# 1/den of each head spread over its 32 feature partitions by a DMA from a DRAM table, in place of selector matmuls

## The chip, the cores and the metric

The kernel runs on one core of one Trainium2 chip. The metric is the device time of one execution in microseconds (us). The core has five engines that run their own instruction streams: PE (TensorE, matmuls), DVE (VectorE), ACT (ScalarE), POOL (GpSimd) and SP (SyncE, which here only issues DMAs). PEld is PE's weight load, which overlaps the matmuls. SPq is the stream of DMA issues of SP.

## What is computed

One transformer block on x of 2048 tokens by 1024 features, with a modulation from a conditioning vector: a linear-attention half and a gated FFN half, each behind a layer norm.

```python
q, k, v = split(h @ wqkv)                    # 32 heads of 32 features
phi = lambda t: where(t > 0, t + 1, exp(t)) + 1e-06
kv  = einsum('bhsd,bhse->bhde', phi(k), v)
z   = einsum('bhsd->bhd', phi(k))
num = einsum('bhqd,bhde->bhqe', phi(q), kv)
den = einsum('bhqd,bhd->bhq', phi(q), z)[..., None] + 1e-06
x   = x + ga * ((num / den) @ wo)
h   = layernorm(x) * (1 + cb) + sb
x   = x + gb * ((gelu(h @ w_gate) * (h @ w_up)) @ w_down)
```

The change is about the division by `den`: one number for each of 32 heads and 2048 tokens.

## The kernel before

The tokens are cut into 16 chunks of 128 and into 4 supergroups (sg) of 512. phi(q) lies transposed in `PQ[sg]`: partitions are features, 128 at a time, so that one of the 8 groups g holds 4 heads of 32 features each, and the free axis is 512 tokens. The output projection reads `PQ`, 128 features by 128 tokens, against `W2`, which is kv times wo. So 1/den must multiply `PQ` before `wo_chunk` (L934) reads it, and 1/den of a head has to stand on all its 32 feature partitions.

Every engine runs a list of instructions in the order in which the program text adds them; a small scheduler (`Sched`, L145) adds the waits from byte ranges that are read and written, in SBUF and in PSUM. SP's DMAs take 8 lanes in turn: a DMA waits for the one issued 8 before it on SP to have landed (`Sched.dma`, L184). An instruction that waits holds everything behind it on its engine.

The stretch that the change touches lies between the last k/v chunk and the FFN:

1. `den(0, 3)` (L858): 32 small matmuls give den of supergroups 0 and 1, for 32 heads by 256 tokens on 32 partitions, four times (i = 0 to 3 is the 256-token half). DVE adds 1e-6 (L868) and takes the reciprocal (L869) into `RDC` [128, 256] f32. POOL splits it into a bf16 high part and a bf16 rest, `RDHL` (L870, L871).
2. Eight rounds u: `q_next` is a q block of 8 matmuls (L654) of supergroup 3, evacuated by ACT's exp (L602) and two DVE instructions (L603, L605), out of two PSUM banks in turn; `w2_pair(u)` is two matmuls (L851) and a copy by ACT (L853). After rounds 0, 2, 4 and 5 comes `bcast(0, r)` (L874): 16 matmuls (L879) of a 0/1 selector `SEL` with `RDHL` that write 1/den on 128 partitions of PSUM banks 4 to 7, and four DVE multiplications `pq_scale` (L888, L892) of `PQ` by PSUM.
3. Twelve output chunks `wo_chunk(0)` to `wo_chunk(11)`, 16 matmuls each (L939), into banks 0/1 or 2/3 in turn (chunk 0: 6/7), each evacuated by one DVE addition into x (L946, here "x1"). A chunk's matmuls wait for the x1 of the chunk two before it. After chunk 0 comes `den(1, 4)` for supergroups 2 and 3, after chunks 2, 3, 5 and 6 `bcast(1, r)`. `ln2_a` (L963) normalises chunks 0 to 3 on ACT with small POOL instructions, and transposes each into `H2[0]` by a DMA from SP (L529, "T2"). After chunk 9, `mod2` (L554) modulates `H2[0]` on DVE in 16 instructions (L539).
4. The FFN of supergroup 0 starts: 28 feature chunks of 16 matmuls (L1005, L1008) in 14 pairs fp, the last four output chunks being put after pairs 1 to 4 by `hooks`. The weights come by `stream_pair` (L928: `WG`, `WU`, 512 KB each, three slots), issued two pairs ahead.

SP's list in this stretch: wg and wu of pairs 0 and 1 (slots which held `WO`, so each waits for some `w2_pair`), `wd_dma` 4, 5 and 6 (L924, 1 MB each, down-projection weights), T2 of chunks 0 to 3, wg and wu of pair 2, and so on. `wd_dma` 0 to 3 follow in the FFN, after pairs 5 to 8.

`SEL` is built once at the start of the program by `sel_build` (L693): 32 matmuls and one ACT copy, amid `warm` matmuls (L667) on zeros, while the first inputs are still on their way.

Of the kernel before, what the change touches and what calls it, by code (L numbers as in the profile page):

```python
# [10 lines left out]
P = 128  # L11
# [39 lines left out]
OFF_VS = OFF_PK + 5 * 2048  # L51
OFF_MS3 = OFF_VS + 3 * NG * KV_SLOT * 2
OFF_XH2 = OFF_MS3 + 8192
OFF_RDHL = OFF_WS + 16384
assert OFF_XH2 + 2048 <= OFF_WS
OFF_GAB = OFF_CONST
OFF_GBB = OFF_CONST + 4096
# [157 lines left out]
def bass_adaLN_cond__linear_attn_block__geglu_ffn__prompt_kernel(  # L215
# [11 lines left out]
):  # L227
    bf16, f32, i32 = dt.bfloat16, dt.float32, dt.int32
    scr_row = nc.dram_tensor("scr_row", [2, 4, 512], f32).ap()
    with ExitStack() as es:  # L230
        es.enter_context(nc.allow_non_contiguous_dma(reason="1024 modulation values, laid out by partition"))
        arena = es.enter_context(nc.sbuf_tensor("arena", [P, ARENA_BYTES], dt.uint8, align_bytes=64))
# [4 lines left out]
        def at(name, shape, dty, off):  # L237
            return nc.alloc_sbuf_tensor_at(name, shape, dty, offset=ABASE + off, align_bytes=4)
# [20 lines left out]
        WMQ = [at(f"wmq{i}", [P, NDC, 2, 256], bf16, MSO[i]) for i in range(4)]  # L259
        WARM = at("warm", [P, 512], bf16, OFF_GUH)  # L260
        WO = at("wo", [P, NDC, D], bf16, OFF_WS)
        RDHL = at("rdhl", [P, 2, 2, SGW // 2], bf16, OFF_RDHL)
        YT = at("yT", [P, NFC, SGW], bf16, OFF_YT)
        WG = [at(f"wg{i}", [P, NDC, 256], bf16, OFF_WS + i * 8192) for i in range(3)]
        WU = [at(f"wu{i}", [P, NDC, 256], bf16, OFF_WS + i * 8192 + 4096) for i in range(3)]
# [18 lines left out]
        _o = OFF_SMALL  # L284
        _small = {}
        for name, shape, dty, sz in [
            ("ident", [P, P], bf16, 256), ("bmask", [P, P], bf16, 256), ("bm32", [P, NG, NH], bf16, 512), ("sel", [P, NG, P], bf16, 2048),
            ("z32", [P, NG, NH], bf16, 512), ("rdc", [P, SGW // 2], f32, 1024),
            ("silr", [P, NDC, 32], bf16, 512),
            ("c8", [NDC, P], bf16, 256), ("cT", [P, NDC], f32, 64), ("chalf", [P, NDC], f32, 64),  # L290
            ("thc", [P, NDC], f32, 64), ("siluT", [P, NDC], bf16, 64), ("modt", [P, 16], f32, 64), ("add4", [P, 4], f32, 64),
            ("sbT", [P, NDC], f32, 64), ("cb1T", [P, NDC], f32, 64),
            ("cbT", [P, NDC], f32, 64), ("zcols", [P, NG], f32, 64), ("neghalf", [P, 1], f32, 64),
            ("st", [P, NCH, 12], f32, NCH * 48), ("mv", [P, NCH, 2], f32, NCH * 8),
            ("rs", [P, NCH], f32, 64), ("nm", [P, NCH], f32, 64), ("ve", [P, NCH], f32, 64),
        ]:
            SMO[name] = _o
            SMSZ[name] = sz
            _small[name] = at(name, shape, dty, _o)
            _o += sz  # L300
        assert _o <= OFF_CONST + SZ_CONST, (_o, OFF_CONST + SZ_CONST)
        IDENT, BMASK, BM32, Z32, SEL = (_small[k] for k in ("ident", "bmask", "bm32", "z32", "sel"))
        RDC = _small["rdc"]
        SILR, C8, CT, CHALF, THC, SILUT = (_small[k] for k in ("silr", "c8", "cT", "chalf", "thc", "siluT"))
        SBT, CB1T, CBT, ZCOLS = (_small[k] for k in ("sbT", "cb1T", "cbT", "zcols"))
# [4 lines left out]
        def r_sm(name):  # L310
            return [(SMO[name], SMO[name] + SMSZ[name], name)]
# [43 lines left out]
        def r_wm(i):  # L355
            return [(MSO[i], MSO[i] + 8192, f"wmst{i}")]

        def r_rdhl(sg, k):
            return [(OFF_RDHL + (sg * 2 + k) * 512, OFF_RDHL + (sg * 2 + k + 1) * 512, "rdhl")]

        R_SEL = r_sm("sel")

        def r_yt(fc, s0=0, s1=SGW):
            return [(OFF_YT + (fc * SGW + s0) * 2, OFF_YT + (fc * SGW + s1) * 2, "yT")]
# [18 lines left out]
        def pr(b):  # L383
            return [(b * 2048, (b + 1) * 2048)]
# [20 lines left out]
        def pset_writer(b, o):  # L405
            for t_ in pr(b):
                sch.ps.set_writer(t_[0], t_[1], o)
# [4 lines left out]
        def gop(fn, **kw):  # L412
            d_ = [last_g[0]] if last_g[0] is not None else []
            last_g[0] = sch.op(G, fn, deps=d_, **kw)
# [9 lines left out]
        bm32f = BM32.ap().rearrange("p a b -> p (a b)")  # L424
        for k in range(HPG):
            gop(lambda e, k=k: e.memset(BMASK[32 * k:32 * (k + 1), 32 * k:32 * (k + 1)], 1.0), wr=r_sm("bmask"))
            gop(lambda e, k=k: e.memset(bm32f[32 * k:32 * (k + 1), k:k + 36 * 7 + 1:36], 1.0), wr=r_sm("bm32"))


        sch.dma(Q, lambda e: e.dma_start(C8[:], c_v), wr=r_sm("c8"), note="c8")  # L430
# [236 lines left out]
        def warm(n, bank=None):  # L667
            for _ in range(n):
                sch.op(T, lambda e: e.matmul(PS(0 if bank is None else bank), WARM[:, 0:P], WARM[:, :], start=bank is not None,
                                             stop=bank is not None, skip_group_check=True),  # L670
                       rd=R_WARM, pwr=pr(bank) if bank is not None else (), note="warm")
# [18 lines left out]
                        kv_mm(c_, "k", jg, b, [dc])  # L690


        def sel_build():  # L693
            o = None
            for g in range(NG):
                b, c0 = 2 + g // 4, (g % 4) * P
                for j in range(4):
                    o = sch.op(T, lambda e, g=g, b=b, c0=c0, j=j: e.matmul(
                        ps_all[32 * j:32 * (j + 1), b * 512 + c0:b * 512 + c0 + P], BM32[:, g, :], IDENT[:, :], start=True, stop=True),
                        rd=r_sm("bm32") + r_sm("ident"), pwr=pr(b) if g % 4 == 0 and j == 0 else (), note=f"sel{g}.{j}")  # L700
                pset_writer(b, o)
            sch.op(A, lambda e: e.activation(SEL[:].rearrange("p a b -> p (a b)"), ps_all[:, 1024:2048], ACTF.Copy),
                   prd=pr(2) + pr(3), wr=R_SEL, note="sel")

        warm(9, 7)
        sel_build()
        ln1_bn(0, 0)
        ln1_bn(0, 1)
        ln1_fin(0)
# [148 lines left out]
        def den(pr_, b):  # L858
            o = None
            for g in range(NG):  # L860
                for i in range(4):
                    sg, t0 = 2 * pr_ + i // 2, (i % 2) * HW
                    o = sch.op(T, lambda e, g=g, i=i, sg=sg, t0=t0: e.matmul(  # L863
                        ps_all[32 * i:32 * (i + 1), b * 512:b * 512 + HW], Z32[:, g, :], PQ[sg][:, g, t0:t0 + HW],
                        start=(g == 0), stop=(g == NG - 1)),
                        rd=r_sm("z32") + r_pq(sg, g, g + 1, t0, t0 + HW), pwr=(pr(b) if g == 0 else ()), note=f"den{pr_} {g}.{i}")
            pset_writer(b, o)
            sch.op(V, lambda e: e.tensor_scalar(RDC[:, :], PS(b, 0, HW), 1e-6, None, op0=ALU.add), prd=pr(b), wr=r_sm("rdc"), note=f"dene{pr_}")  # L868
            sch.op(V, lambda e: e.reciprocal(RDC[:, :], RDC[:, :]), rd=r_sm("rdc"), wr=r_sm("rdc"), note=f"rden{pr_}")  # L869
            o = sch.op(G, lambda e: e.tensor_copy(RDHL[:, pr_, 0, :], RDC[:, :]), rd=r_sm("rdc"), wr=r_rdhl(pr_, 0), deps=[last_g[0]], note=f"rdhi{pr_}")  # L870
            last_g[0] = sch.op(G, lambda e: e.tensor_tensor(RDHL[:, pr_, 1, :], RDC[:, :], RDHL[:, pr_, 0, :], ALU.subtract),  # L871
                   rd=r_sm("rdc") + r_rdhl(pr_, 0), deps=[o], wr=r_rdhl(pr_, 1), note=f"rdlo{pr_}")

        def bcast(pr_, r):  # L874
            o = [None] * 4
            for gi in range(2):
                for k in range(2):
                    for i in range(4):
                        o[i] = sch.op(T, lambda e, gi=gi, k=k, i=i: e.matmul(  # L879
                            PS(4 + i, gi * HW, (gi + 1) * HW), SEL[32 * i:32 * (i + 1), 2 * r + gi, :], RDHL[32 * i:32 * (i + 1), pr_, k, :],  # L880
                            start=(k == 0), stop=(k == 1)),
                            rd=R_SEL + r_rdhl(pr_, k), pwr=(pr(4 + i) if gi == 0 and k == 0 else ()), note=f"bc{pr_} {r}.{gi}.{k}.{i}")
            for i in range(4):
                pset_writer(4 + i, o[i])
            for i in range(4):
                pq_scale(pr_, r, i)

        def pq_scale(pr_, r, i):  # L888
            sg, t0 = 2 * pr_ + i // 2, (i % 2) * HW
            ap = PQ[sg][:, 2 * r:2 * r + 2, t0:t0 + HW]  # L890
            rng = r_pq(sg, 2 * r, 2 * r + 2, t0, t0 + HW)
            sch.op(V, lambda e: e.tensor_tensor(ap, ap, PS(4 + i).rearrange("p (a b) -> p a b", a=2), ALU.mult),  # L892
                   prd=pr(4 + i), rd=rng, wr=rng, note=f"pqs{pr_}.{r}.{i}")

        q_todo += [(NSG - 1, qc) for qc in range(NG)]
        qn = [0]
# [11 lines left out]
        q_evac(*first_q)  # L908
        q_next()
        den(0, 3)  # L910
        kvbd()
        q_next()
        q_next()
        kvt()
        for u in range(NG):
            q_next()
            w2_pair(u)
            if u in (0, 2, 4, 5):
                bcast(0, (0, 2, 4, 5).index(u))
        assert not q_todo  # L920

        wd_q = [0]
# [53 lines left out]

        stream_pair(0, 0)
        stream_pair(0, 1)
        for q in (4, 5, 6):
            wd_dma(q)  # L980
        for c_ in range(12):
            wo_chunk(c_, 6 if c_ == 0 else 2 * (c_ % 2))
            if c_ == 0:
                den(1, 4)
            if c_ in (2, 3, 5, 6):
                bcast(1, (2, 3, 5, 6).index(c_))
            if c_ < 4:
                ln2_a(c_, False)
            if c_ == 9:
                mod2(0, 2)  # L990
                mod2(2, 2)
# [57 lines left out]

        for ci in range(CPG):  # L1050
            hook(0, 1 + ci, lambda ci=ci: wo_chunk(12 + ci, 6))
        for q in range(4):
            hook(0, 5 + q, lambda q=q: wd_dma(q))
        for sg in range(NSG):
# [94 lines left out]
```

## Time and profile before

| what | value |
|---|---|
| median of 8 runs | 849.27 us (849.08 to 849.71) |
| the profiled execution's own time | 849.27 us |
| its span, first to last instruction | 847.5 us |
| granted TensorE clock | 1.00 of full speed |
| DVE busy | 492.1 us (58%) |
| ACT busy | 295.8 us (35%) |
| POOL busy | 25.4 us (3%) |
| DMA, mean over the span | 123 GB/s, 104.06 MB |
| selector matmuls, 128 | 5.5 us busy, 270 ns each |
| `pq_scale`, 32 | 19.8 us busy, 680 ns each |
| reciprocal, 2 | 3.5 us busy, 1753 ns each |
| first `den` matmul, first `wo_chunk` matmul, first FFN matmul | 178.7, 205.2 and 250.3 us from the span's start |

Times of the profile are from the start of the span. In a line of the timeline the columns are start, duration of the whole group, engine, line, operation, names, shape and count, and in brackets how long the engine had been idle and what ended that. Matmuls are pipelined: the mean of one (379 ns for 512 columns) is longer than the step from one start to the next (0.216 us), so costs on PE are taken from starts. In a line by windows, "DMA share" is the mean busy share of the 16 DMA engines (it can pass 1 in a short window) and the last column is GB/s.

### The profile page before, as it was taken

The page shows a single profiled execution, that of the slowest core. Times are in us where ns is not written, and L with a number is a line of the kernel's source. Part 1 is how long each engine was busy: PE and PEld are TensorE (multiplying, and loading weights), DVE is VectorE, ACT ScalarE, POOL GpSimd, SP SyncE. Part 2 cuts the span into 40 slices and gives each one's busy share as a digit, 9 for nine tenths or more (in the row PEclk, how much of TensorE's full clock was granted, in tenths as well). Part 3 has the DMA queues.
Part 4 walks back from the last instruction along what each step waited for, and adds up shares of the span by engine and source line. Part 5 has one row for each costly group of instructions (what it writes and reads, how often), then busy time and mean ns, then how long its engine had stood idle before and what let it go on. Part 6 is the DMA issues. An engine that isn't in the chain of part 4 may idle for free.

```text
span 847.5 us, 11598 instructions
## 1 busy us (share of the span) xinstructions
PE 840.8 (99%) x4386; PEld 390.2 (46%) x4386; DVE 492.1 (58%) x883; ACT 295.8 (35%) x484; POOL 25.4 (3%) x68
## 2 busy tenths in 40 slices
PE   8999999999999999999999999999999999999998
PEld 4454444444444444444444444444444444444445
DVE  5676767778665555563456555445666535556512
ACT  3343333344504345430254452035444204544300
POOL 2000000000200000010000001000000000000000
PEclk9999999999999999999999999999999999999999
DMA  9991823004423388341455534055553305555000
GB/s 276 358 285 26 261 56 95 13 2 152 135 63 100 101 253 242 100 100 37 112 150 151 154 108 104 21 147 156 154 150 100 75 19 155 150 151 148 6 19 26
DMA packets 179927, 104.06 MB, mean 123 GB/s; under 512 B 32536, under 2 KB 171928, under 8 KB 179872
## 3 DMA queue, kind: packets, MB, share of 16 engines
q1 hardware_dynamic: 179872, 103.33, 43.8%
q8 instruction: 35, 0.57, 0.3%
q14 instruction: 20, 0.16, 0.1%
HBM read 92.28 MB, written 4.21 MB: 114 GB/s over the span
## 4 chain that ended last, share of the span: by engine, by line
PE 97%; DMA 1%; SPq 1%; DVE 1%; issue 0%; ACT 0%; ACTq 0%
PE ps_all L1033 23%; PE ps_all L1008 23%; PE ps_all L1005 23%; PE ps_all L613 13%; PE ps_all L939 7%; PE ps_all L654 6%; DMA wk<-in_A_wqkv_dram 1%; PE ps_all L635 1%; PE ps_all L879 0%; SPq L444 0%; PE ps_all L585 0%; SPq L433 0%; PE ps_all L851 0%; DVE pq L892 0%; PE ps_all L863 0%; PE ps_all L566 0%
## 5 line engine op out<-in xcount | busy, mean ns | idle before, releaser
L1005 PE MATMUL ps_all<-h2T,wg 128*128 128x512 bf16 x896 | 339.6, 379 | 0.0
L1008 PE MATMUL ps_all<-h2T,wu 128*128 128x512 bf16 x896 | 339.6, 379 | 0.0
L1033 PE MATMUL ps_all<-wd,yT 128*128 128x512 bf16 (+1 forms) x924 | 194.1, 373 | 0.0
L1016 ACT ACTIVATE q<-ps_all 128x512 f32<-128x512 f32 x112 | 66.9, 597 | 235.3 <-PE ps_all L1005 234.0
L1033 PEld LDWEIGHTS ps_all<-wd,yT 128*128 128x128 bf16 x924 | 90.4, 98 | 103.3
L1005 PEld LDWEIGHTS ps_all<-h2T,wg 128*128 128x128 bf16 x896 | 87.7, 98 | 105.8 <-issue 0.2
L1008 PEld LDWEIGHTS ps_all<-h2T,wu 128*128 128x128 bf16 x896 | 87.7, 98 | 105.6
L1018 DVE SCALAR_TENSOR_TENSOR ww<-q,ps_all 128x512 f32<-128x512 f32 x112 | 77.0, 688 | 92.5 <-ACT guh L1017 92.5
L1021 DVE SCALAR_TENSOR_TENSOR ww<-th,guh 128x512 f32<-128x512 f32 x112 | 77.5, 692 | 77.9 <-ACT th L1020 77.9
L1020 ACT ACTIVATE th<-ww 128x512 f32<-128x512 f32 x112 | 70.5, 629 | 84.4 <-DVE ww L1018 84.4
L1023 DVE TENSOR_TENSOR yT<-ww,ps_all 128x512 bf16<-128x512 f32 x112 | 76.9, 686 | 3.8
L1038 DVE TENSOR_TENSOR ps_all<-ps_all,gbb 128x512 f32<-128x512 f32 (+1 forms) x33 | 22.5, 682 | 94.8 <-PE ps_all L1033 94.8
L1017 ACT ACTIVATE guh<-ps_all 128x512 f32<-128x512 f32 x112 | 66.3, 592 | 0.0
L602 ACT ACTIVATE eb<-ps_all 128x512 f32<-128x512 f32 x64 | 37.5, 601 | 81.0 <-PE ps_all L613 38.5
L613 PE MATMUL ps_all<-wk,h1T 128*128 128x512 bf16 x256 | 58.2, 379 | 0.9 <-DMA wk<-in_A_wqkv_dram 0.9
L654 PE MATMUL ps_all<-h1T,wq 128*128 128x512 bf16 x256 | 58.9, 379 | 0.0
L613 PE MATMUL ps_all<-wv,h1T 128*128 128x512 bf16 x256 | 57.7, 379 | 0.0
L939 PE MATMUL ps_all<-w,pq 128*128 128x512 bf16 x256 | 56.9, 379 | 0.0
L603 DVE TENSOR_SCALAR eb<-eb 128x512 f32<-128x512 f32 x64 | 27.1, 424 | 32.9 <-ACT eb L602 32.4
L613 PEld LDWEIGHTS ps_all<-wk,h1T 128*128 128x128 bf16 x256 | 24.7, 98 | 30.4 <-DVE h1T L539 2.1
L613 PEld LDWEIGHTS ps_all<-wv,h1T 128*128 128x128 bf16 x256 | 25.0, 98 | 29.7 <-DVE eb L603 0.2
L939 PEld LDWEIGHTS ps_all<-w,pq 128*128 128x128 bf16 x256 | 24.6, 98 | 30.1 <-issue 1.1
(88 smaller groups left out, 409.4 us busy)
## 6 DMA issues: line engine op xcount, KB each, us to landing
wg<-in_B_w_gate_dram SPq DMA_DIRECT2D x56, 512.0 KB, 4.0
wu<-in_B_w_up_dram SPq DMA_DIRECT2D x56, 512.0 KB, 5.2
wmst<-in_w_mod_dram SPq DMA_DIRECT2D x8, 1024.0 KB, 11.9
wd<-in_B_w_down_dram SPq DMA_DIRECT2D x7, 1024.0 KB, 7.6
wmq<-in_w_mod_dram SPq DMA_DIRECT2D x8, 512.0 KB, 6.9
out_dram<-xall SPq DMA_DIRECT2D x31, 128.0 KB, 1.7
xall<-in_A_x_dram SPq DMA_DIRECT2D x3, 1024.0 KB, 11.6
wk<-in_A_wqkv_dram SPq DMA_DIRECT2D x4, 512.0 KB, 7.7
```

What stands on the lines that cost most here:

```text
L613: o = sch.op(T, lambda e, dc=dc: e.matmul(PS(bank), H1[sg][:, dc, ci * P:(ci + 1) * P], W_[:, dc, jg * 512:(jg + 1) * 512], start=(dc == 0 ...
L654: o = sch.op(T, lambda e, dc=dc: e.matmul(PS(b), WQ[:, dc, qc * P:(qc + 1) * P], H1[sg][:, dc, :], start=(dc == 0), stop=(dc == NDC - 1)), ...
L939: last[half] = sch.op(T, lambda e, g=g, half=half: e.matmul(PS(b0 + half), PQ[sg][:, g, ci * P:(ci + 1) * P], W2[:, g, half * 512:(half + ...
L1005: og = sch.op(T, lambda e, dc=dc: e.matmul(PS(bg), WG[slot][:, dc, e_ * P:(e_ + 1) * P], H2[sg][:, dc, :], start=(dc == 0), stop=(dc == ND ...
L1008: ou = sch.op(T, lambda e, dc=dc: e.matmul(PS(bu), WU[slot][:, dc, e_ * P:(e_ + 1) * P], H2[sg][:, dc, :], start=(dc == 0), stop=(dc == ND ...
L1016: sch.op(A, lambda e: e.activation(Q1[j][:, :], PS(bg), ACTF.Square, scale=math.sqrt(GELU_A)), prd=pr(bg), wr=rq, note=f"q1 {fc}")
L1017: ogh = sch.op(A, lambda e: e.activation(GUH[j][:, :], PS(bg), ACTF.Copy, scale=0.5), prd=pr(bg), wr=rg, note=f"gh {fc}")
L1018: sch.op(V, lambda e: e.scalar_tensor_tensor(WW[j][:, :], Q1[j][:, :], 1.0, PS(bg), op0=ALU.add, op1=ALU.mult), rd=rq, prd=pr(bg), wr=rw, ...
L1020: sch.op(A, lambda e: e.activation(TH[j][:, :], WW[j][:, :], ACTF.Tanh, scale=GELU_C), rd=rw, wr=rt, note=f"th {fc}")
L1021: sch.op(V, lambda e: e.scalar_tensor_tensor(WW[j][:, :], TH[j][:, :], 1.0, GUH[j][:, :], op0=ALU.add, op1=ALU.mult), rd=rt + rg, wr=rw, n ...
L1023: sch.op(V, lambda e: e.tensor_tensor(YT[:, fc, :], WW[j][:, :], PS(bu), ALU.mult), rd=rw, prd=pr(bu), wr=r_yt(fc), note=f"yT {fc}")
L1033: o = sch.op(T, lambda e, b=b, fc=fc, c0=c0, c1=c1, n=n: e.matmul(PS(b, 0, n), YT[:, fc, ci * P:(ci + 1) * P], WDT[fc // 4][:, fc % 4, c0:c1],
```

## The change

- `SEL`, `sel_build`, `RDHL`, its two POOL instructions and `bcast` with its 128 selector matmuls go. Three more `warm` matmuls stand where `sel_build` was.
- After each reciprocal, SP stores `RDC` (128 KB, f32) to a DRAM table `scr_rd` (one such store for supergroups 0 and 1, one for 2 and 3). The heads' order within den's 32 partitions is changed (the memset of `BM32`) so that the 8 groups' values of one position k in the group lie in one row of 8 KB.
- `rb_load(sg)`: eight DMAs, for each 256-token half h and each k one that reads a row of 8 KB 32 times into 32 partitions of `RB[sg % 2]` (f32; 256 KB for each DMA, 2 MB for each supergroup). The two buffers lie where `WV` was, and where `PK` and `VS` were. Only the first DMA of a half carries the waits of the buffer; all eight wait for the store.
- `pq_scale(sg, h)`: four DVE multiplications of `PQ` (bf16) by `RB` (f32, in SBUF), of the same 512 elements for each partition as before, but ordered by half and supergroup: those of supergroup 0 after rounds 3 and 5, of 1 after chunks 0 and 1, of 2 after chunks 4 and 5, of 3 after chunks 6 and 7. They wait for all four DMAs of their half.
- On SP: store 0, `rb_load(0)`, `rb_load(1)`, then wg and wu of pairs 0 and 1, store 1, `rb_load(2)`, T2 of chunk 0, `rb_load(3)`, T2 of chunks 1 to 3, wg and wu of pair 2. `wd_dma` 4, 5 and 6 move into the FFN, after pairs 1, 2 and 3.

```diff
-        def sel_build():
...
-        warm(9, 7)
-        sel_build()
+        warm(12, 7)
...
-            o = sch.op(G, lambda e: e.tensor_copy(RDHL[:, pr_, 0, :], RDC[:, :]), rd=r_sm("rdc"), wr=r_rdhl(pr_, 0), deps=[last_g[0]], note=f"rdhi{pr_}")
-            last_g[0] = sch.op(G, lambda e: e.tensor_tensor(RDHL[:, pr_, 1, :], RDC[:, :], RDHL[:, pr_, 0, :], ALU.subtract),
-                   rd=r_sm("rdc") + r_rdhl(pr_, 0), deps=[o], wr=r_rdhl(pr_, 1), note=f"rdlo{pr_}")
-
-        def bcast(pr_, r):
...
+            o_s = sch.dma(Q, lambda e: e.dma_start(scr_rd[2 * pr_:2 * pr_ + 2].rearrange("s f k (g t) -> (s f k g) t", g=NG), RDC[:, :]),
+                          rd=r_sm("rdc"), note=f"rden{pr_}.st")
+            o_rd[pr_] = o_s
...
+        def rb_load(sg):
+            i = sg % 2
+            for h in range(2):
+                made = []
+                for k in range(HPG):
+                    made.append(sch.dma(Q, lambda e, h=h, k=k: e.dma_start(
+                        RB[i][32 * k:32 * (k + 1), h, :, :].rearrange("p a b -> p (a b)"),
+                        scr_rd[sg, h, k:k + 1, :].to_broadcast([32, NG * HW])),
+                        wr=r_rb(i, h) if k == 0 else (), deps=made[0].deps if k else [o_rd[sg // 2]], note=f"rb{sg}.{h}.{k}"))
+                rb_ops[sg, h] = made
+
+        def pq_scale(sg, h, gs=((0, 2), (2, 4), (4, 6), (6, 8))):
+            i, t0 = sg % 2, h * HW
+            for g0, g1 in gs:
+                ap = PQ[sg][:, g0:g1, t0:t0 + HW]
+                rng = r_pq(sg, g0, g1, t0, t0 + HW)
+                sch.op(V, lambda e, ap=ap, i=i, h=h, g0=g0, g1=g1: e.tensor_tensor(ap, ap, RB[i][:, h, g0:g1, :], ALU.mult),
+                       rd=rng + r_rb(i, h, g0, g1), wr=rng, deps=rb_ops[sg, h], note=f"pqs{sg}.{h}.{g0}")
...
         den(0, 3)
+        rb_load(0)
+        rb_load(1)
         kvbd()
...
-            if u in (0, 2, 4, 5):
-                bcast(0, (0, 2, 4, 5).index(u))
+            if u in (3, 5):
+                pq_scale(0, (u - 3) // 2)
...
         stream_pair(0, 1)
-        for q in (4, 5, 6):
-            wd_dma(q)
         for c_ in range(12):
             wo_chunk(c_, 6 if c_ == 0 else 2 * (c_ % 2))
             if c_ == 0:
                 den(1, 4)
-            if c_ in (2, 3, 5, 6):
-                bcast(1, (2, 3, 5, 6).index(c_))
+                rb_load(2)
+            if c_ in (0, 1):
+                pq_scale(1, c_)
+            if c_ == 1:
+                rb_load(3)
+            if c_ in (4, 5, 6, 7):
+                pq_scale(2 + (c_ - 4) // 2, c_ % 2)
             if c_ < 4:
                 ln2_a(c_, False)
...
+        for q in range(3):
+            hook(0, 1 + q, lambda q=q: wd_dma(4 + q))
```

More of the change, by code (lines that the diff above doesn't have):

```diff
@@ L53 @@
 OFF_XH2 = OFF_MS3 + 8192
-OFF_RDHL = OFF_WS + 16384
+OFF_RB = [OFF_WD + 16384, OFF_YT]
 assert OFF_XH2 + 2048 <= OFF_WS
@@ L229, in bass_adaLN_cond__linear_attn_block__geglu_ffn__prompt_kernel @@
     scr_row = nc.dram_tensor("scr_row", [2, 4, 512], f32).ap()
+    scr_rd = nc.dram_tensor("scr_rd", [NSG, 2, HPG, NG * (SGW // 2)], f32).ap()
     with ExitStack() as es:
@@ L261, in bass_adaLN_cond__linear_attn_block__geglu_ffn__prompt_kernel @@
         WO = at("wo", [P, NDC, D], bf16, OFF_WS)
-        RDHL = at("rdhl", [P, 2, 2, SGW // 2], bf16, OFF_RDHL)
+        RB = [at(f"rb{i}", [P, 2, NG, SGW // 2], f32, OFF_RB[i]) for i in range(2)]
         YT = at("yT", [P, NFC, SGW], bf16, OFF_YT)
@@ L286, in bass_adaLN_cond__linear_attn_block__geglu_ffn__prompt_kernel @@
         for name, shape, dty, sz in [
-            ("ident", [P, P], bf16, 256), ("bmask", [P, P], bf16, 256), ("bm32", [P, NG, NH], bf16, 512), ("sel", [P, NG, P], bf16, 2048),
+            ("ident", [P, P], bf16, 256), ("bmask", [P, P], bf16, 256), ("bm32", [P, NG, NH], bf16, 512),
             ("z32", [P, NG, NH], bf16, 512), ("rdc", [P, SGW // 2], f32, 1024),
@@ L301, in bass_adaLN_cond__linear_attn_block__geglu_ffn__prompt_kernel @@
         assert _o <= OFF_CONST + SZ_CONST, (_o, OFF_CONST + SZ_CONST)
-        IDENT, BMASK, BM32, Z32, SEL = (_small[k] for k in ("ident", "bmask", "bm32", "z32", "sel"))
+        IDENT, BMASK, BM32, Z32 = (_small[k] for k in ("ident", "bmask", "bm32", "z32"))
         RDC = _small["rdc"]
@@ L356, in r_wm, with r_rb @@
             return [(MSO[i], MSO[i] + 8192, f"wmst{i}")]
-        def r_rdhl(sg, k):
-            return [(OFF_RDHL + (sg * 2 + k) * 512, OFF_RDHL + (sg * 2 + k + 1) * 512, "rdhl")]
-        R_SEL = r_sm("sel")
+        def r_rb(i, h, g0=0, g1=NG):
+            return [(OFF_RB[i] + (h * NG + g0) * 1024, OFF_RB[i] + (h * NG + g1) * 1024, f"rb{i}")]
         def r_yt(fc, s0=0, s1=SGW):
@@ L426, in bass_adaLN_cond__linear_attn_block__geglu_ffn__prompt_kernel @@
             gop(lambda e, k=k: e.memset(BMASK[32 * k:32 * (k + 1), 32 * k:32 * (k + 1)], 1.0), wr=r_sm("bmask"))
-            gop(lambda e, k=k: e.memset(bm32f[32 * k:32 * (k + 1), k:k + 36 * 7 + 1:36], 1.0), wr=r_sm("bm32"))
+            gop(lambda e, k=k: e.memset(bm32f[32 * k:32 * (k + 1), 8 * k:8 * k + 33 * 7 + 1:33], 1.0), wr=r_sm("bm32"))
         sch.dma(Q, lambda e: e.dma_start(C8[:], c_v), wr=r_sm("c8"), note="c8")
@@ L690, in k_part @@
                         kv_mm(c_, "k", jg, b, [dc])
-        def sel_build():
[L694 to L703, printed above, removed]
-        warm(9, 7)
-        sel_build()
+        warm(12, 7)
         ln1_bn(0, 0)
@@ L874, in bcast @@
-        def bcast(pr_, r):
[L875 to L893, printed above, removed]
+            o_s = sch.dma(Q, lambda e: e.dma_start(scr_rd[2 * pr_:2 * pr_ + 2].rearrange("s f k (g t) -> (s f k g) t", g=NG), RDC[:, :]),
+                          rd=r_sm("rdc"), note=f"rden{pr_}.st")
@@ new lines, in den @@
+            o_rd[pr_] = o_s
+        o_rd = {}
+        rb_ops = {}
+        def rb_load(sg):
[8 more added lines that the diff above has]
+                rb_ops[sg, h] = made
```

## The prediction

> **What bounds the kernel now.** I read first the busy times, then the chain of waits, then PE's timeline over the stretch that the change touches.
>
> ```profile
> PE 840.8 (99%) x4386; PEld 390.2 (46%) x4386; DVE 492.1 (58%) x883; ACT 295.8 (35%) x484; POOL 25.4 (3%) x68
> PE 97%; DMA 1%; SPq 1%; DVE 1%; issue 0%; ACT 0%; ACTq 0%
> ```
>
> PE works 99% of the span, and 97% of the chain that ends last is PE. So what is taken from PE's list shortens the run one for one, until another engine or a transfer is late. Next, how PE's list passes one selector round among the q blocks, the one that waits, and one among the output chunks:
>
> ```profile
> 195.84 0.59 PE L851 MATMUL ps_all<-wo,kvt 128*128 128x512 bf16 x2
> 196.36 0.62 PE L879 MATMUL ps_all<-rdhl,sel 32*128 32x256 bf16 x16
> 196.91 1.90 PE L654 MATMUL ps_all<-h1T,wq 128*128 128x512 bf16 x8
> 198.65 0.59 PE L851 MATMUL ps_all<-wo,kvt 128*128 128x512 bf16 x2
> 199.17 0.28 PE L879 MATMUL ps_all<-rdhl,sel 32*128 32x256 bf16 x2
> 199.72 0.28 PE L879 MATMUL ps_all<-rdhl,sel 32*128 32x256 bf16 x1 [0.27 <-DVE pq L892]
> 200.32 0.61 PE L879 MATMUL ps_all<-rdhl,sel 32*128 32x256 bf16 x13 [0.32 <-DVE pq L892]
> 200.86 1.90 PE L654 MATMUL ps_all<-h1T,wq 128*128 128x512 bf16 x8
> 216.74 0.62 PE L879 MATMUL ps_all<-rdhl,sel 32*128 32x256 bf16 x16
> 217.28 3.63 PE L939 MATMUL ps_all<-w,pq 128*128 128x512 bf16 x16
> 233.06 17.44 PE L939 MATMUL ps_all<-w,pq 128*128 128x512 bf16 x80
> 250.33 0.38 PE L1005 MATMUL ps_all<-h2T,wg 128*128 128x512 bf16 x1
> ```
>
> Step by starts: a w2 pair with no round behind it takes 0.43 (the next q block starts 0.43 after it), with a round 1.07. An output chunk takes 3.45 (17.27 for five of them, 233.06 to 250.33). The fourth round also waits for PSUM that the multiplications of the round before still read.
>
> **What goes from PE.** Rounds after u = 0, 2 and 4: 0.64 each; after u = 5: 2.21 - 0.43 = 1.78; four among the chunks, 0.65 each by the starts (for instance 216.74 - 209.72 - 6.91 + 0.54). Together 1.92 + 1.78 + 2.62 = 6.3 us.
>
> **The start.** sel_build's 32 matmuls take 0.97 of PE (6.21 to 7.18); three warm ones take 0.65 (0.216 each, as after 8 us) to 1.28 (0.427 each, as before 6 us), so between -0.3 and +0.3. I take 0: PE waits at 18.33 for a transfer of wk anyway; uncovered it would be those 0.3. ACT's copy of 1.02 us goes, which had nothing late behind it.
>
> **Multiplications.** The nearest row with the same operands (bf16 by f32, both in SBUF) is the fold of wo, twice as long; half of 1218 is 609, and the present row is 680. I take 680 each, and 2.5 for four in a row as now (2.47). Count 32 stays; only the order changes.
>
> ```profile
> L821 DVE TENSOR_TENSOR wo<-wo,gab 128x1024 bf16<-128x1024 bf16 x8 | 9.4, 1218 | 0.0
> L892 DVE TENSOR_TENSOR pq<-pq,ps_all 128x512 bf16<-128x512 bf16 x32 | 19.8, 680 | 0.0
> L946 DVE TENSOR_TENSOR xall<-ps_all,xall 128x1024 bf16<-128x1024 f32 x16 | 19.6, 1222 | 14.4 <-PE ps_all L939 14.4
> ```
>
> After u = 3 the four lie on DVE from about 194.3 to 196.8; the q evacuation behind them frees its bank at 197.9, while PE wants it at 197.1 and goes on at 198.0: a new stall of 0.9. So if no transfer is late, chunk 0 starts at 205.19 - 3.70 + 0.9 = 202.4, and the FFN at 202.4 + 12 x 3.45 + 1.07 (den) = 244.9 in place of 250.33: **5.4 us less**, the most that there is.
>
> **The transfers.** Eight MB of broadcast are new on SP's queue. The nearest rows are the broadcasts of gab and gbb (DRAM rows read by 128 partitions):
>
> ```profile
> gab<-scr_row SPq DMA_DIRECT2D x1, 512.0 KB, 10.4
> gbb<-scr_row SPq DMA_DIRECT2D x1, 512.0 KB, 8.7
> 98.00:100.00 2.00, 2.00 (x11) 0.90 (x10) 1.39 (x3) 0.60 (x1) 0.00 (x0) 1.00 1.05 426
> ```
>
> Their landing times hold a queue of weights ahead of them; the rate when they flow is 426 GB/s. Each new transfer reaches a quarter of the partitions. If that costs nothing, the rate is 426; if rate goes with partitions reached, 426/4 = 107. No row has a large transfer to fewer than 128 partitions. I take the middle in ratio, **213 GB/s** (an estimate): 1 MB, a half of a supergroup, in 4.92 us.
>
> [...]
>
> Now the chain, at 213. The reciprocal ends at 181.03 + 1.75 = 182.78; store to the next DMA's issue 1.9 (for mrow and sbT: 119.36 to 121.29), so 184.8; first bytes 1.4 after an issue (wg: 189.39 to about 190.8), 186.2. The halves of supergroups 0 and 1 flow until 191.1, 196.0, 201.0 and 205.9, and land 0.6 later (as T2 did: flow to 220.4, landed 221.0). They are due at 194.3, 199.0, 209.7 and 213.4: in time, by 2.4 or more. Behind them on SP's queue wg and wu of pairs 0 and 1, 2 MB at 300 GB/s (1.03 MB in 3.4 us from 237), 7.0 us, to 212.9. Behind those store 1, issued at 209.7 already (chunk 0 ends 205.85, den 0.99, then x1, the addition and 1.75): landed at 213.9. Supergroup 2 flows from 215.4 to 225.2, its halves landing at 220.9 and 225.8, due 222.2 and 226. Then T2 of chunk 0, 1.4; supergroup 3 from 226.6 to 236.5, landing at **232.1 and 237.1**. Due are they at 229.7 and, after the shift, 235.8.
>
> So DVE waits twice, and behind it stand the x1 additions that free PSUM. The multiplications end at 234.6, x1 of chunk 7 at 235.8, chunk 9 starts at 236.0 (PE ready 234.55). The second set ends at 239.6, x1 of chunk 8 at 240.8, chunk 10 runs from 241.0, chunk 11 to 247.9, and the FFN starts at 248.0. T2 of chunks 1 to 3 queue behind: 240.7, landed 241.3; mod2 (4.2) is due at 242.0: hidden, by under 1 us. Two other waits of these DMAs do not bind: the buffers are free before the loads come (multiplications of supergroup 0 done at 201.5, load at 214.0; of 1 at 215.9, load behind T2), and a lane's DMA of eight before has landed while seven others, 8.6 us of flow, are still queued. Gain 250.33 - 248.0 = **2.3 us**.
>
> The 8 MB are paid in full along this chain, so the FFN starts at 248.0 + 39.4 x (213/rate - 1): break-even is 201 GB/s, the full 5.4 is had from 231 on.
>
> **At nothing.** wd 4 to 6 leave a queue that moved 402 GB/s from 212 to 216 and go behind pairs 1 to 3: the windows from 264 to 295 move some 100 GB/s, and pairs 6 and 7 carry the same 1 MB beside wg and wu in 7 us (306 GB/s, PE never idle). Were that cover gone, each would cost up to its 2.6 us at 402. POOL's split (1.07 twice) is off the path.
>
> **The sum.** The profiled execution took 849.27 (span 847.5 and 1.8 around it), which is also the median. 849.27 - 2.3 = **847.0**.
>
> **Rivals.**
> The first: transfers as fast as gab's, over 231 GB/s. For it: the sources repeat in both, and rows of 8 KB are longer than gab's 2 KB. Against: only 32 partitions. 849.27 - 5.4 = 843.9.
> The second, slower: under 201 GB/s the last half of supergroup 3 holds DVE at its multiplication, x1 of chunk 8 behind it and PE behind that, for longer than the selector rounds cost. For it: 32 short transfers instead of few long ones, and the queue never drains between 186 and 240. At 175: 256.6, so 849.27 + 6.2 = 855.5.
> The third: rate by partitions, 107. FFN at 287, 886. [...]
>
> **Chances.** Forecast (201 to 231 GB/s, 843.9 to 849.3) 0.43; as fast as gab 0.13; 150 to 201 (849.3 to 863) 0.36; below that 0.08. A measurement here tells 0.2%, 1.7 us, from no change: that is 210 GB/s upward and 193 downward. Of the forecast 0.29 lies above 210 and 0.14 within; of the slower rival 0.06 within. Faster 0.42, same 0.20, slower 0.38. The range runs from 843.7 to 858 (167 GB/s), leaving out the quarter rate and the low end of the second rival; the forecast's own is 843.9 to 849.3.
>
> **What would show it.** PE passes u = 5 with no wait and chunk 0 starts near 202.4; L879 is gone. In windows from 187 to 205 the DMA rate is near 213, with share near 1. Half 1 of supergroup 3 lands near 237; DVE waits for it; chunk 9 or 10 waits for x1; the FFN starts near 248. I am wrong if the rate is elsewhere, if the first halves are late among the q blocks, if T2 is late for mod2, or if the FFN's first pairs wait for weights.

## The result, and the profile after

| | before | after |
|---|---|---|
| median | 849.39 us (35 runs, 848.68 to 852.61) | 847.08 us (13 runs, 846.58 to 849.17) |
| profiled execution, own time and span | 849.27, 847.5 us | 848.07, 846.3 us |
| first `den` matmul | 178.72 us | 179.77 us |
| first FFN matmul | 250.33 us | 249.03 us |
| from the one to the other, "the stretch" | 71.61 us | 69.26 us |

The ratio is 0.9972, with a 95% interval of 0.9965 to 0.998: 2.3 us less, and 847.0 was forecast. The interval alone leaves 1.7 to 3.0 us, so that the two agree within 0.1 us is closer than the runs can tell.

The stretch is the better measure of what the change does. In the profiled execution of after, PE waited 1.03 us at 34.69 for a VectorE instruction, where before has no wait, and everything behind it lies some 1 us later. Such differences at the start come and go: among the eleven kernels from after to e10 (ten have after's start, e8 the old one) the first `den` matmul lies between 177.90 and 180.30 us. Below, 1.05 us (179.77 - 178.72) is taken off times of after where they are set against the forecast.

The page of after, busy times and chain of waits:

```profile
PE 835.6 (99%) x4229; PEld 387.3 (46%) x4229; DVE 492.0 (58%) x883; ACT 295.0 (35%) x483; POOL 24.5 (3%) x64
PE 93%; DMA 4%; DVE 2%; SPq 1%; issue 1%; ACT 0%; DVEq 0%; ACTq 0%
```

PE has 5.2 us less to do, and the span did not become shorter by as much. The chain tells why: DMA holds 4% of it where it held 1%, DVE 2% where it held 1%. The end is no longer set by PE alone. PE's timeline over the stretch (start, duration of the group, engine, line, operation, count, and in brackets the idle time before it and what ended it):

```profile
197.74 0.59 PE L837 MATMUL ps_all<-wo,kvt 128*128 128x512 bf16 x2
198.99 1.90 PE L653 MATMUL ps_all<-h1T,wq 128*128 128x512 bf16 x8 [0.66 <-DVE pq L604]
200.73 0.59 PE L837 MATMUL ps_all<-wo,kvt 128*128 128x512 bf16 x2
...
203.32 3.62 PE L928 MATMUL ps_all<-w,pq 128*128 128x512 bf16 x16
...
207.86 27.80 PE L928 MATMUL ps_all<-w,pq 128*128 128x512 bf16 x128
237.22 3.63 PE L928 MATMUL ps_all<-w,pq 128*128 128x512 bf16 x16 [1.56 <-DVE xall L935]
242.11 7.08 PE L928 MATMUL ps_all<-w,pq 128*128 128x512 bf16 x32 [1.27 <-DVE xall L935]
249.03 0.38 PE L997 MATMUL ps_all<-h2T,wg 128*128 128x512 bf16 x1
```

No selector matmul stands between a w2 pair and what follows. In their place are three waits: 0.66 among the q blocks, and 1.56 and 1.27 before chunks 9 and 10, where PE wants a PSUM bank that x1 (now L935) has not yet emptied. What x1 stands behind is seen on DVE, in the multiplications of supergroups 2 and 3:

```profile
223.02 2.49 DVE L879 TENSOR_TENSOR pq<-pq,rb 128x512 bf16<-128x512 bf16 x4
...
227.54 2.50 DVE L879 TENSOR_TENSOR pq<-pq,rb 128x512 bf16<-128x512 bf16 x4 [0.90 <-DMA rb<-scr_rd]
...
233.53 2.50 DVE L879 TENSOR_TENSOR pq<-pq,rb 128x512 bf16<-128x512 bf16 x4 [2.35 <-DMA rb<-scr_rd]
...
238.42 2.50 DVE L879 TENSOR_TENSOR pq<-pq,rb 128x512 bf16<-128x512 bf16 x4 [1.26 <-DMA rb<-scr_rd]
```

DVE waits 4.5 us in all for the loads of 1/den, and PE feels 2.8 of it. The same in the page's groups (busy, mean ns of one, idle time and its releaser), then its DMA line (KB each, us from issue to landing), then a window over the loads of supergroups 0 and 1 (last two columns: DMA share and GB/s):

```profile
L879 DVE TENSOR_TENSOR pq<-pq,rb 128x512 bf16<-128x512 bf16 x32 | 19.9, 683 | 4.5 <-DMA rb<-scr_rd 4.5
L928 PE MATMUL ps_all<-w,pq 128*128 128x512 bf16 x256 | 56.6, 379 | 2.8 <-DVE xall L935 2.8
```

```profile
rb<-scr_rd SPq DMA_DIRECT2D x32, 256.0 KB, 9.0
```

```profile
188.00:204.00 16.00, 15.35 (x72) 6.81 (x71) 12.42 (x23) 10.64 (x15) 0.00 (x0) 1.00 1.02 221
```

All 16 DMA engines are busy (share 1.02) and move 221 GB/s, about half of the 426 of gab's broadcast (share 1.05, before, 98 to 100). SP's timeline shows where the second set of loads starts:

```profile
207.79 1.68 SPq L921 DMA_DIRECT2D wu<-in_B_w_up_dram  x1
210.53 0.72 SPq L856 DMA_DIRECT2D scr_rd<-rdc  x1
215.10 3.58 SPq L868 DMA_DIRECT2D rb<-scr_rd  x8
```

Store 1 is issued at 210.53, and the first load behind it, which waits for it to have landed, at 215.10: 4.6 us. For store 0 the same takes 1.7 (183.92 to 185.63).

### The profile page after: what moved, and what is told of

It reads as the page before. It is cut to its first block, busy times and chain, and to the rows that moved or that the text cites. A ratio compares the mean times of both kernels' runs of the same rounds, so it can differ in the third digit from the quotient of the medians.

```text
span 846.3 us, 11333 instructions
## 1 busy us (share of the span) xinstructions
PE 835.6 (99%) x4229; PEld 387.3 (46%) x4229; DVE 492.0 (58%) x883; ACT 295.0 (35%) x483; POOL 24.5 (3%) x64
## 4 chain that ended last, share of the span: by engine, by line
PE 93%; DMA 4%; DVE 2%; SPq 1%; issue 1%; ACT 0%; DVEq 0%; ACTq 0%
PE ps_all L1025 23%; PE ps_all L1000 23%; PE ps_all L997 23%; PE ps_all L612 13%; PE ps_all L653 6%; PE ps_all L928 3%; DMA rb<-scr_rd 1%; DMA h2T<-xh 1%; PE ps_all L634 1%; DMA xall<-in_A_x_dram 1%; DVE pq L879 1%; DMA scr_rd<-rdc 1%; PE ps_all L584 0%; SPq L868 0%; PE ps_all L565 0%
```

## The experiments

The theory: PE would give 5.4 us, but the loads of 1/den, slow (221 GB/s) because each reaches only 32 partitions, come late for the last two supergroups, and that gives 3 us back. Rivals: the rate is that of any broadcast, or of the queue, and the loss lies elsewhere (the store, the stall among the q blocks, the moved weights, the start). All kernels are edits of the kernel after, and every one was timed in five rounds beside the kernel before.

| kernel | median, us | ratio to before, 95% interval | stretch, us |
|---|---|---|---|
| after | 847.08 | 0.9972 (0.9965 to 0.998) | 69.26 |
| e1_rows128 | 843.83 | 0.9934 (0.9921 to 0.9946) | 66.08 |
| e2_wd_back | 854.89 | 1.0065 (1.0052 to 1.0077) | 77.06 |
| e3_store_act | 846.78 | 0.9970 (0.9960 to 0.9981) | 69.24 |
| e4_order | 845.08 | 0.9951 (0.9939 to 0.9964) | 67.40 |
| e5_split | 846.54 | 0.9966 (0.9955 to 0.9977) | 69.46 |
| e6_rows128_split | 843.32 | 0.9923 (0.9906 to 0.9939) | 65.25 |
| e7_bf16 | 843.10 | 0.9920 (0.9905 to 0.9936) | 65.25 |
| e8_sel_start | 847.51 | 0.9968 (0.9957 to 0.9979) | 68.53 |
| e9_pair1_late | 845.35 | 0.9939 (0.9920 to 0.9957) | 67.42 |
| e10_all_f32 | 843.24 | 0.9915 (0.9897 to 0.9934) | 65.31 |

The stretch comes from one execution each. e8 has the same instructions in it as after and is 0.73 us shorter, so smaller differences of it are not read as effects of an edit.

### e1: the same bytes to 128 partitions

```diff
-                        RB[i][32 * k:32 * (k + 1), h, :, :].rearrange("p a b -> p (a b)"),
-                        scr_rd[sg, h, k:k + 1, :].to_broadcast([32, NG * HW])),
+                        RB[i][:, h, 2 * k:2 * k + 2, :].rearrange("p a b -> p (a b)"),
+                        scr_rd[sg, h, 0:1, 2 * HW * k:2 * HW * (k + 1)].to_broadcast([P, 2 * HW])),
```

> Same 32 loads of 256 KB, in the same order and queue, but each fills all 128 partitions with 2 KB of one row (the values of k = 0 go to every partition, so the scaling is left out for three heads of four), in place of 32 partitions with 8 KB. Theory (the rate goes with the partitions that one transfer reaches, and this rate sets when the FFN starts): the loads flow at over 350 GB/s in place of some 217, no multiplication waits for a load, no output chunk waits for an addition into x, the FFN starts near 244.9 us from the span's start, and the time is near 843.9. Rival (the rate is low because these are many short transfers, or because they read the same row again and again): the rate stays near 217 and the time near 847.1. Second rival (the stretch is set by DVE's groups of four multiplications and not by the loads): the rate rises, but the time stays within 0.5 of 847.1.

It took 843.83 us. The window over the first loads, and PE's chunks:

```profile
188.00:204.00 16.00, 15.34 (x72) 6.83 (x71) 12.37 (x22) 10.58 (x14) 0.00 (x0) 1.00 1.05 318
```

```profile
206.52 38.16 PE L928 MATMUL ps_all<-w,pq 128*128 128x512 bf16 x176
```

The rate over the same window is 318 GB/s in place of 221: it rises from 241 to 392 in windows of 2 us from 188 to 198, so the 350 that was expected is passed only at the end of the loads (behind them the window holds weights). No multiplication waits for its load, and chunks 1 to 11 run in one piece. Number of transfers, their size, their queue and their place are those of after; what has changed is the number of partitions that each reaches and, with it, the length of a row (2 KB here, 8 KB in after). So the 221 GB/s belongs to the form of the transfer, and the 3 us that the change did not give are lost there. This run does not part the partitions from the row's length; e7, with rows of 4 KB to 32 partitions, says more on that. Here store 1 is followed by its first load after 1.7 us (209.20 to 210.93), which e9 comes back to.

### e2: the down-projection weights back ahead of store 1

```diff
         stream_pair(0, 1)
+        for q in (4, 5, 6):
+            wd_dma(q)
...
-        for q in range(3):
-            hook(0, 1 + q, lambda q=q: wd_dma(4 + q))
```

> The three loads of wd, 3 MB, stand again where they stood before the change, ahead of the second store on SP's queue. Theory (store, loads and weights go through one queue in order, and the loads' end sets the FFN's start): 3 MB at 402 GB/s put 7.8 us ahead of the second store, the second half of supergroup 3 lands some 7.8 us later, and the time is 854 to 855. Rival (the order on the queue doesn't matter, because the loads are not what the stretch waits for): within 0.5 of 847.1.

It took 854.89 us, slower than before. SP's timeline, and the first multiplication of supergroup 2 on DVE:

```profile
212.18 0.75 SPq L856 DMA_DIRECT2D scr_rd<-rdc  x1
222.86 2.19 SPq L868 DMA_DIRECT2D rb<-scr_rd  x5
```

```profile
229.91 2.50 DVE L879 TENSOR_TENSOR pq<-pq,rb 128x512 bf16<-128x512 bf16 x4 [7.59 <-DMA rb<-scr_rd]
```

Store 1 now takes 10.7 us, and the stretch grows by 77.06 - 69.26 = 7.8 us, three times the 2.6 for which the forecast priced one such transfer without cover. Moving them is the part of the change without which the whole of it loses. In the FFN, where after issues them (257.0, 263.9, 274.3), PE never waits.

PE's wait of 5.63 us before chunk 7 comes with a lower clock, from within the wait on: 0.82 in the window from 230 to 232, 0.50 in the three from 232 to 238. In the window's line the third column from the end is the granted clock:

```profile
233.60 9.29 PE L928 MATMUL ps_all<-w,pq 128*128 128x512 bf16 x32 [5.63 <-DVE xall L935]
234.00:236.00 2.00, 2.00 (x6) 0.76 (x5) 1.36 (x3) 0.49 (x1) 0.00 (x0) 0.50 1.18 270
```

Chunks 7 and 8 take 9.29 us in place of 7.08. Chunks 9 and 10 still have to wait behind them (1.49 and 1.12 us), for x1 additions that stand behind multiplications waiting for loads (2.43 and 1.11 us), so the 7.8 us are still the loads'.

### e3: store 1 issued by ScalarE

```diff
-            o_s = sch.dma(Q, lambda e: e.dma_start(scr_rd[2 * pr_:2 * pr_ + 2].rearrange("s f k (g t) -> (s f k g) t", g=NG), RDC[:, :]),
+            o_s = sch.dma(A if pr_ else Q, lambda e: e.dma_start(scr_rd[2 * pr_:2 * pr_ + 2].rearrange("s f k (g t) -> (s f k g) t", g=NG), RDC[:, :]),
```

> Only the second store is issued by ACT instead of SP, so that it isn't queued behind wg and wu of the first two pairs. Theory (the store's place in the queue, 4.6 us from its issue at 210.5 to the first load at 215.1 where the first store took 1.7, is part of the chain that sets the FFN's start): the first load of supergroup 2 is issued 2 to 2.9 us earlier, the waits of the multiplications shrink from 4.5 us to about 2, and the time falls by 1.5 to 2.7, to 844.4 to 845.6. Rival (what waits is ACT: the store's wait for the reciprocal stands ahead of the layer norm of chunk 0, whose transposes become late for the modulation): no gain, 847 or more.

It took 846.78 us with a stretch of 69.24: nothing gained. ACT's timeline, then SP's:

```profile
209.30 0.34 ACTq L856 DMA_DIRECT2D scr_rd<-rdc  x1
```

```profile
213.84 3.60 SPq L868 DMA_DIRECT2D rb<-scr_rd  x8
```

The store is issued by another engine, and still 4.5 us pass to the first load, which comes 35.26 us behind the first `den` matmul (35.33 in after). So it was not SP's list that held the store. In after it was issued at once too: the reciprocal ends at 210.45, the store goes at 210.53. Nor was ACT late, as the rival had it: T2 of chunk 0 is issued 38.96 us behind the first `den` matmul (39.02 in after). e9 shows what the store stood behind.

### e4: the four loads of a half in the order 0, 2, 1, 3

```diff
-                for k in range(HPG):
+                for k in (0, 2, 1, 3):
```

> The four loads of a half go in the order k = 0, 2, 1, 3 instead of 0, 1, 2, 3; all else is the same. [...] Rival (neighbours in the queue overlap where they write different halves of the partitions): the rate rises clearly above 217, towards 300 or more, and the time falls by 1.5 to 3, to 844 to 845.6.

Loads that follow each other now reach the lower and the upper 64 partitions in turn. The rival stood against an expectation of no change by the order (near 217 GB/s, 846.8 to 847.4). Neither was right as a whole: the rate rose a little, to 229 GB/s in the window below (221 in after), where the rival asked for 300, but the time fell into the rival's range, to 845.08 us, 2.0 less than after.

```profile
188.00:204.00 16.00, 15.35 (x72) 6.80 (x71) 12.37 (x22) 10.58 (x14) 0.00 (x0) 1.00 1.01 229
```

By the forecast's slope, 39.4 x 213 x (1/221 - 1/229) = 1.3 us of it come from the rate, an estimate; the stretch is 1.9 shorter, and what made the rest was not tried. The rise itself is clear of scatter: in the same window five kernels with the old order and 256 KB loads to 32 partitions (after, e2, e3, e8, e9) move 219 to 223 GB/s, the two with the new order 229 and 230 (e10). At this point of the slope the 2.0 us are nearly as much as the 2.3 that the change itself brought.

### e5 and e6: the first multiplications split, with slow and with fast loads

```diff
-            if u in (3, 5):
-                pq_scale(0, (u - 3) // 2)
+            if u == 3:
+                pq_scale(0, 0, ((0, 2), (2, 4)))
+            if u == 4:
+                pq_scale(0, 0, ((4, 6), (6, 8)))
+            if u == 5:
+                pq_scale(0, 1)
```

e5 is this alone, e6 this together with e1's edit.

> The four multiplications that stand after round 3 are split: two after round 3, two after round 4; the loads are as in the changed kernel. Theory (while the loads set the FFN's start, a stall ahead of them is free): PE's idle 0.66 before the q block of round 6 goes and chunk 0 starts some 0.6 earlier, but the waits of chunks 9 and 10 grow by as much, the FFN starts as before and the time is 846.7 to 847.5. Rival (PE's own list still decides, and each stall on it counts): 846.3 to 846.6.

> The same split on the kernel whose loads fill 128 partitions (the scaling is left out for three heads of four, as there). Theory (with the loads out of the way PE's list decides, so the same edit now counts): 0.5 to 0.8 less than the 843.83 of the kernel without the split, 843.0 to 843.3. Rival (the stall is made up later in any case): no difference, 843.6 to 844.0.

The stall of 0.66 among the q blocks is gone in both. In e5 the stretch stays (69.46 against 69.26): what PE gains there it waits for longer in front of chunk 9 (2.35 us in place of 1.56), which starts 57.41 us behind the first `den` matmul, 57.45 in after.

```profile
235.31 12.22 PE L932 MATMUL ps_all<-w,pq 128*128 128x512 bf16 x48 [2.35 <-DVE xall L939]
```

The theory had the wait in front of chunk 10 grow too; it is gone instead, and not to PE's gain. After the longer wait the first 13 of the 48 matmuls, from 235.31 to 239.81, go at 0.346 us each where 0.216 is the full pace (the mean granted clock of this execution is 0.998, that of after 1.00), and chunks 9 to 11 take 12.22 us where 10.5 is their full pace (3 x 3.45, and the last matmul's end). From chunk 9 to the FFN pass 12.05 us, 11.81 in after. e5's median, 846.54, lies in the rival's range (846.3 to 846.6), but its runs (846.07 to 848.58) spread wider than theory and rival lie apart, so the theory stands on the stretch and the trace.

In e6, where no load is late, the stretch falls from 66.08 to 65.25 and the median by 0.5 us (the two kernels' runs overlap; the stall that has left PE's timeline is the better evidence). So an improvement ahead of the wait that binds is worth nothing until that wait is gone. With neither stall nor late load left, e6 shows what the matmuls' removal is worth: 71.61 - 65.25 = 6.36 us.

### e7: 1/den in bf16

```diff
-    scr_rd = nc.dram_tensor("scr_rd", [NSG, 2, HPG, NG * (SGW // 2)], f32).ap()
+    scr_rd = nc.dram_tensor("scr_rd", [NSG, 2, HPG, NG * (SGW // 2)], bf16).ap()
...
-        RB = [at(f"rb{i}", [P, 2, NG, SGW // 2], f32, OFF_RB[i]) for i in range(2)]
+        RB = [at(f"rb{i}", [P, 2, NG, SGW // 2], bf16, OFF_RB[i]) for i in range(2)]
...
-            sch.op(V, lambda e: e.reciprocal(RDC[:, :], RDC[:, :]), rd=r_sm("rdc"), wr=r_sm("rdc"), note=f"rden{pr_}")
+            sch.op(V, lambda e: e.reciprocal(RDB[:, :], RDC[:, :]), rd=r_sm("rdc"), wr=r_sm("rdb"), note=f"rden{pr_}")
```

> The reciprocal is written in bf16 and so are the table and its spread copies, so each load is 128 KB to 32 partitions and the whole 4 MB in place of 8 (1/den is rounded to bf16, which leaves out the lower part that was kept before). Theory (bytes over a fixed rate set the FFN's start): at the same 220 GB/s the loads take half of the time, no multiplication waits for one, and the time is that of the unhindered list, 843.8, or down to 842.8 if multiplications of two bf16 operands are faster than 685 ns and so take the 0.66 stall away too. Rival (a fixed cost for each of the 32 loads matters, not its bytes): the rate in GB/s halves, the waits stay, 846 to 847.

Half the bytes, and the loads are never late: 843.10 us, stretch 65.25. The multiplications became shorter too, since both operands are bf16 now:

```profile
L880 DVE TENSOR_TENSOR pq<-pq,rb 128x512 bf16<-128x512 bf16 x32 | 11.3, 416 | 0.0
```

That is 416 ns in place of 683, and with shorter multiplications the stall among the q blocks goes without a split. The first loads' rate, in a window with the DMA engines all busy:

```profile
190.00:192.00 2.00, 2.00 (x11) 0.91 (x10) 1.05 (x2) 1.51 (x2) 0.00 (x0) 1.00 1.00 232
```

From 186 to 194 such windows give 232 to 244 GB/s. Half the row's length at the same 32 partitions thus moves the rate by 5 to 10%, so the length of a row can hardly be what took e1 to 318; the partitions reached are the likelier cause, though rows of 2 KB to 32 partitions were not tried.

### e8: sel_build back at the start

```diff
-        warm(12, 7)
+        warm(9, 7)
+        sel_build()
```

> The selector is built again at the start, 32 matmuls and a copy by ACT in place of three warm matmuls, and nothing reads it. Theory (the start waits for its inputs, so this part of the change is worth nothing): within 0.4 of 847.1. Rival (some of the gain came from the start): 0.5 to 1.3 more, 847.6 to 848.4.

It took 847.51 us, 0.43 above after, in neither range; its runs (846.19 to 848.59) cover after's median, and the ratio to the kernel before, 0.9968, is no higher than after's 0.9972. What the change saves at the start is too small to be told from nothing here.

### e9: one weight pair behind the loads

```diff
-        stream_pair(0, 1)
         for c_ in range(12):
...
+        stream_pair(0, 1)
         stream_pair(0, 2)
```

> The load of the FFN weight pair 1 (wg and wu, 1 MB together) is moved from ahead of store 1 to behind the attention's last 1/den loads, just ahead of pair 2. The theory (store 1's table can only land when the weight transfers queued ahead of it on the same 16 DMA engines have drained; the first load after it came 4.6 us behind its issue, against 1.7 us for store 0): 1 MB less ahead of the store, so its first load comes 2.4 to 3.5 us earlier against the first den matmul, and den matmul to first FFN matmul falls from 69.3 to 66.5-67.0 us, time 844.3 to 845.0. Rival: the store is slow for itself, whatever is ahead of it (4.5 us again), and the stretch stays at 69.0-69.5, time 846.5 to 847.2. Second rival: pair 1's weights, now late, stop the FFN at its second pair; the FFN's first matmul is earlier but a PE wait on wg or wu of more than 1 us appears behind it and the time is not below 846.

It took 845.35 us, with a stretch of 67.42: the theory's mechanism, but 0.4 us outside both of its ranges. SP's timeline:

```profile
209.73 0.34 SPq L856 DMA_DIRECT2D scr_rd<-rdc  x1
211.45 3.58 SPq L868 DMA_DIRECT2D rb<-scr_rd  x8
```

The store takes 1.7 us, as store 0 does. So the 4.6 us were the weights still moving on the DMA engines when it was issued, and that answers e3 as well. No wait for wg or wu appears in the FFN. The first load came 2.85 us earlier against the first `den` matmul, but only 1.84 of that reached the FFN. One load of supergroup 3 is the eighth DMA after T2 of chunk 0 and waited 2.3 us for T2 to land (0.6 in after), during which the queue ran low:

```profile
224.00:226.00 2.00, 2.00 (x11) 0.87 (x9) 2.00 (x4) 0.40 (x2) 0.00 (x0) 1.00 0.71 138
```

That this wait is the missing 1.0 us was not tried by itself.

### e10: the edits of e4, e5 and e9 together, in f32

> Full computation in f32, three edits together: the weight pair 1 behind the 1/den loads, the order of the four loads of a chunk pair turned to 0,2,1,3, and the four multiplications of a round split two and two over two places. Theory: with store 1 landing earlier and the loads some 5 per cent faster, no multiplication waits for its 1/den by more than 1 us, so what is left is the removal of the selector matmuls alone: den matmul to first FFN matmul 65.25 to 66.2 us (65.25 was left where nothing waited), time 843.0 to 844.2. Rival: the loads' rate, still below 250 GB/s, leaves two waits of 1 us or more on the last chunks; stretch 67 or more, time 845 or more.

It took 843.24 us (842.59 to 844.11), 6.1 us under before, with 1/den kept in f32 as in after. PE's timeline:

```profile
206.30 38.22 PE L932 MATMUL ps_all<-w,pq 128*128 128x512 bf16 x176
```

Chunks 1 to 11 run in one piece. DVE still waits twice for loads (0.37 and 1.11 us, the second 0.1 longer than the theory allowed), and no x1 is late enough for PE to feel it. The stretch is 65.31, as in e6 and e7: three ways to take the loads from the path end at the same place, which is the removal of the selector matmuls and no more.

## Why the prediction was right, point by point

**PE.** 6.3 us was read from starts in the timeline; e6 and e7 leave 6.36. The stall after the four multiplications was put at 0.9 and is 0.66. Chunk 0 was expected at 202.4 and starts at 203.32 - 1.05 = 202.27.

**Multiplications.** 680 ns was taken, 683 measured, from SBUF as from PSUM.

**The start** was taken as nothing; e8 shows no difference clear of the spread. That spread, 2.4 us between the profiled executions, is larger than the 0.3 that the forecast allowed for.

**The rate** was the number with the widest bounds, 107 to 426, and the middle of the two in ratio, 213, was a choice and not a reading. It is 221 in the first window and lower later (197 to 201 in windows of 2 us from 228 to 234). That the choice came so near is part luck: near 221 the forecast's slope is 39.4 x 213 / 221 / 221 = 0.17 us for each GB/s. By the forecast's formula 221 throughout would have put the FFN at 246.6 and not at the 248.0 found; the lower rate later goes the other way. e1 (318 in the first window) shows that the form of the transfer makes the rate, and with e7 (232 to 244) that it is more likely the partitions reached than the length of the rows.

**The chain of transfers.** Less 1.05, the first load of supergroup 2 is issued at 214.05 (213.9 was the landing of its store). The second half of supergroup 2 is there at 226.5 (225.8), the halves of 3 at 232.5 and 237.4 (232.1 and 237.1); chunk 9 starts at 236.2 (236.0), chunk 10 at 241.1 (241.0), the FFN at 248.0 (248.0). DVE waits three times and not twice, the first time 0.9 us, which PE does not feel. `mod2` begins at 242.05 (242.0) and stays hidden.

**Waits that were said not to bind.** The loads waited 7.5 us in all for earlier loads' lanes. Meanwhile the DMA share stayed near 1, so this should cost nothing, as the forecast said, though it was not tried by itself; e9 has one such wait, behind T2, during which the share fell to 0.71.

**The weights at nothing.** Right, with the cover's price of 2.6 each confirmed by e2.

**The rivals.** "As fast as gab" was 843.9, and e1, whose loads pass the 231 GB/s that this rival asked for, takes 843.8. The slower rival's mechanism, a half of supergroup 3 holding DVE, x1 and PE in that order, is what happens in after too, for both halves, only to the extent of 2.8 us and not of more than the selector rounds cost. e2 shows it beyond that point.

## What to carry to other kernels

Work taken from the engine that bounds is worth its time only as far as what takes its place arrives in time: walk the new transfers along their queue with a rate for their own form, and count what is ahead of them on the DMA engines, from whichever engine it was issued (store 1 took 4.6 us issued by SP in after, 4.5 by ACT in e3, and 1.7 with 1 MB less ahead in e9). Where the end hangs on a transfer, look first at the partitions that it reaches (318 GB/s for 128 against 221 for 32 here), its bytes (with half of them no load was late), and what is queued ahead of it; a stall earlier on the path is worth nothing before that (0.66 us off PE left the stretch of e5 as it was, and took 0.83 from it in e6). Compare stretches between two fixed instructions when the start of a program varies by as much as the effect.

## What the runs showed of the hardware

- 256 KB loads to 32 partitions kept all 16 DMA engines busy (share 1.02) at 221 GB/s (after), those to 128 partitions moved 318 in the same window (share 1.05) and up to 392 in windows of 2 us (share 1.03, e1). Here busy engines were no sign of the full rate.
- Turning the order so that neighbours in the queue reach different halves of the partitions gave 4% (229 and 230 GB/s in e4 and e10, 219 to 223 without it).
- From the issue of a store of 128 KB to the first load that waits for it, 1.7 us passed when no earlier transfer was still moving (store 0 of after, store 1 of e1 and e9), 4.6 (after), 4.5 (e3, where ACT issued it) and 3.7 (e4) behind the weight pairs 0 and 1, and 10.7 with 3 MB more ahead (e2).
- The VectorE product of bf16 by f32, 128 x 512, took the same from SBUF (683 ns, after) as from PSUM (680, before), and of bf16 by bf16 416 (e7).
- After PE had waited 2.35 us (e5) its next 13 matmuls went at 0.346 us each in place of 0.216; with a wait of 5.63 us (e2) the granted clock was 0.82 and then 0.50 in the windows from 230 to 238, part of them still in the wait, and 0.97 in the next; the waits of 1.56 and 1.27 us in after left it at 1.00.
